# Expert blocks, token shift and weight conversions: one shift buffer for two mixes, five units in another form, a third weight chunk converted later

## The chip, the core and the metric

The kernel runs on one core of a Trainium2 chip. The metric is device time in microseconds, the median of several executions. Of the engines, TensorE appears in the profile as PE (matmuls) and PEld (weight loads), VectorE as DVE, ScalarE as ACT, GpSimd as POOL, and SyncE as SP, which issues nearly all DMAs.

## The reference

Three layers in a row, for 4 sequences of 1088 tokens: an attention with polynomial features, an expert layer with a token shift, and a gated layer with a spatial product over the tokens. All is float32.

```python
# 1 attention, 4 heads of 32: phi(x) = (S1 x) outer (S2 x), 64 features
num = einsum('bhsf,bhfd->bhsd', phi(q), kv)          # kv = sum over s of phi(k) v
x = num / (einsum('bhsf,bhf->bhs', phi(q), z) + 1e-6) # z = sum over s of phi(k)
# 2 expert layer, d 128, d_ff 1024; x_prev is x one token back
xk = mu_k * x + (1 - mu_k) * x_prev
xr = mu_r * x + (1 - mu_r) * x_prev
x = sigmoid(xr @ w_r) * (relu(xk @ w_k) ** 2 @ w_v)
# 3 gated layer
u, v = split(relu(x @ w_in))
v = einsum('ts,bsd->btd', w_spatial, normalised(v)) + b_spatial
out = (u * v) @ w_out
```

## The kernel before

Features lie on the 128 partitions and tokens along the columns. Each sequence is cut into three chunks of 384, 384 and 320 tokens, so there are twelve chunks j = 0 to 11. A float32 product is made from two parts of each operand: a high part H (a copy rounded to the type of the fast matmul) and a low part L, which is the value less H. A *split* product is three matmuls, `mm3` (L131): low by high, high by high, high by low. `copy` (L134) is an ACT pass and makes H; `low` (L137) is a subtraction on DVE or POOL and makes L. A *plain* product is one float32 matmul (L406), which the profile shows as two passes.

**Expert layer.** It runs as 96 units g = 8 j + f: eight blocks f of 128 hidden features for each of twelve chunks. `up(g)` makes a unit's first product into one of three PSUM banks (0, 1, 2, in rotation) and its Relu on ACT (L362). Then the unit is squared in one of three forms, which `kind(g)` takes from the pattern `PAT`:

- P: POOL squares the Relu (L365), ACT makes H by a second square (L394), DVE makes L. The second product is split.
- D: ACT squares into a float32 tile (L382). The second product is plain (L406), with the float32 weights `wvT`.
- Q: DVE multiplies the bank by its Relu (L370), ACT copies to H, POOL makes L. The second product is split.

From unit 26 to 85 even units are P and odd ones D. `down(g)` makes the second product four units after the first (`LAG`) and adds up over the chunk's eight units in one bank. L410 on DVE multiplies the finished chunk by the sigmoid.

**Token shift.** The tile `x` of a sequence holds a zero column and then the tokens, so the token before is the same tile one column to the left. For chunk j `prep(j)` has POOL subtract the two (L318) into the tile `mx` and DVE make the mix xk in place there (L319); then H on ACT and L on DVE. `prep_r(j)` uses `mx` again: ACT scales the token before (L335), DVE adds the other part (L336), ACT makes H and POOL makes L. There is one `mx`. The first chunk (j = 0) makes xk straight from PSUM. `receive(j)` makes the receptance product into one of the three banks of `up`, and `gate(j)` puts its sigmoid (L351) into tile m0 or m1, by j even or odd, where L410 reads it.

**Spatial weights.** They are converted in three chunks of columns, c = 0, 1, 2, with nine row blocks each. One `wstep` converts the block whose load is under way (ACT copy, low part on DVE or POOL by the table `WDVE`; the ninth also takes a second load and copy) and then issues the load of the next block (L434) into one of two tiles, `st0` and `st1`. A load of c = 2 isn't issued by a step before unit 96. `spatial(b, d, c)` are the plain units of the gated layer for the first sequence, twelve of them: four are planned among the last expert units (at 93, 95, 97, 99), eight (u = 4 to 11) follow, of which u = 4 to 7 read c = 0 and 1, and u = 8 is the first to read c = 2. `WB` says how many steps are written into each of them. Where a needed chunk isn't converted, `spatial` makes the missing steps itself first.

**Order.** `plan(g, fn, ...)` puts a helper behind unit g in the order in which the program is written. From the written program the framework's scheduler makes the order of each engine's queue, with each tile's data dependences; an instruction may run well ahead of its written place. `behind` and `late` tie a helper's instructions to earlier ones of the same engine. A tile name (`m0`, `mx`, `st0`) is one buffer: a new use waits until every reader of the old one has finished.

Of the kernel before, what the change touches and what calls it, by code (L numbers as in the profile page):

```python
# [11 lines left out]
AF = mybir.ActivationFunctionType  # L12
ALU = mybir.AluOpType
# [35 lines left out]
ES = 93  # L49
EP = 2  # L50
G2 = (86, 94)
V2 = 3
PAT = ('QD', 'PD', 'PQ', 'PD')
UT = 'x0'
# [2 lines left out]
LAG = 4  # L57
WDVE = ((0, 1), (1, 2), (2, 1), (2, 2), (3, 1), (3, 2), (4, 0), (4, 2), (6, 0), (7, 0), (7, 1), (8, 2))
VD0 = 2
WB = (0, 0, 4, 7, 2, 4, 1, 0)  # L60
NB0 = 9
W1G = 69
W1N = 8
# [21 lines left out]
def attn_moe_gmlp(ctx: ExitStack, tc: tile.TileContext, qT, kT, va, st, wk, wv, wr, win, wout,  # L85
                  wT, wtail, btail, mu, ident, msk, out):
    nc = tc.nc
    TE, VE, SE, GE = nc.tensor, nc.vector, nc.scalar, nc.gpsimd
# [7 lines left out]
    def sb(tag, shape, dt=F32):  # L96
        uid[0] += 1
        return pool.tile(shape, dt, tag=tag, bufs=1, name=f"{tag}_{uid[0]}")
# [12 lines left out]
    def m(i):  # L111
        return f"m{i}"
# [7 lines left out]

    idn = sb("idn", [128, 128])
    mk = sb("mk", [128, 24])
    mus = sb("mus", [128, 4])
    half = sb("half", [128, 1])
    ebias = sb("ebias", [128, 1])
    warm = sb("warm", [128, 1])
# [6 lines left out]
    def copy(dst, src):  # L133
        return SE.activation(out=dst, in_=src, func=AF.Copy)  # L134

    def low(eng, L, src, H):
        return eng.tensor_tensor(out=L, in0=src, in1=H.bitcast(F32), op=ALU.subtract)  # L137
# [27 lines left out]
    def load64(src, H, L, o, n):  # L165
        raw = sb(f"w{rot(*[-x for x in CVT]) * -1}", [128, n, 2], I32)
        nc.sync.dma_start(out=flat(raw), in_=src[:, o:o + n].bitcast(I32))
        pending_raw.append((raw, n, H[:, o:o + n], L[:, o:o + n]))
# [12 lines left out]
    q_s, k_s, v_s, kbd, xTs, kps, qst = {}, {}, {}, {}, {}, {}, {}  # L181
# [123 lines left out]
    anchor, prep_L, xk_op = [None, None, None], [None, None], [None]  # L305
    RA = [m(i) for i in (2, 3, 4, 5, 6, 7)]
    RB = [m(i) for i in (2, 3, 4)]
    xks, sgs, sqs, vvs, hls = {}, {}, {}, {}, {}
    x_last = [None]

    def prep(i):
        b, c = divmod(i, 3)
        o, n = CH[c]
        xT = xTs[b]
        xp = xT[:, o:o + n]
        xk = d = sb("mx", [128, n])
        if i:
            GE.tensor_tensor(out=d, in0=xT[:, o + 1:o + 1 + n], in1=xp, op=ALU.subtract)  # L318
            VE.scalar_tensor_tensor(out=xk, in0=d, scalar=mus[:, 0:1], in1=xp, op0=ALU.mult, op1=ALU.add)  # L319
        else:  # L320
            px, a = first_x
            xk_op[0] = VE.scalar_tensor_tensor(out=xk, in0=px[:, :n], scalar=mus[:, 0:1], in1=a, op0=ALU.mult, op1=ALU.add)
        H, L = sb(m(11 + i % 2), [128, n], F32R), sb(m(13 + i % 2), [128, n], F32R)
        prep_L[1] = copy(H, xk)
        if not i:
            behind(prep_L[1:], copy, xT[:, 1:1 + n], px[:, :n])
        prep_L[0] = low(VE, L, xk, H)
        xks[i] = (H, L)

    def prep_r(i):  # L330
        b, c = divmod(i, 3)
        o, n = CH[c]
        xp = xTs[b][:, o:o + n]
        xr = sb("mx", [128, n])
        SE.activation(out=xr, in_=xp, func=AF.Copy, scale=mus[:, 3:4])  # L335
        VE.scalar_tensor_tensor(out=xr, in0=xTs[b][:, o + 1:o + 1 + n], scalar=mus[:, 1:2], in1=xr, op0=ALU.mult, op1=ALU.add)  # L336
        H, L = sb("xrH", [128, n], F32R), sb("xrL", [128, n], F32R)
        copy(H, xr)
        low(GE, L, xr, H)
        sgs[i] = (H, L)  # L340
# [13 lines left out]
    def up(g):  # L354
        i, f = divmod(g, NF)
        n = CH[i % 3][1]
        hk = bank(rot(0, 1, 2))[:, :n]
        w = slice(128 * f, 128 * f + 128)
        mm3(hk, wkH[:, w], wkL[:, w], *xks[i], True, True)
        R = RA if g < GL else RB  # L360
        r = sb(rot(*R), [128, n])
        SE.activation(out=r, in_=hk, func=AF.Relu)  # L362
        if kind(g) == "P":
            sq = sb(rot(*R), [128, n])
            anchor[2] = GE.tensor_tensor(out=sq, in0=r, in1=r, op=ALU.mult)  # L365
            sqs[g] = (r, sq)
        elif kind(g) == "D":
            sqs[g] = (r, None)
        else:
            anchor[0] = VE.tensor_tensor(out=r, in0=hk, in1=r, op=ALU.mult)  # L370
            sqs[g] = (None, r)

    def kind(g):
        p = PAT[(g >= G1) + sum(g >= x for x in G2)]
        return p[g % len(p)]

# [171 lines left out]
    def spatial(b, d, c, fill, early=False):  # L548
        while not all((k, c) in done for k in range(NK + 1)):
            was = wi[0], len(pending_raw)  # L550
            wstep()
            assert was != (wi[0], len(pending_raw))
        Hs, Ls, T1, T2 = vnt[b, d]
        xH, xL = xsp[b]
        o, n = CH[c]
        cs, ds = slice(o, o + n), slice(128 * d, 128 * d + 128)
        pu = bank(7 if early else 3)[:, :n]
        mm3(pu, winH[:, ds], winL[:, ds], xH[:, cs], xL[:, cs], True, True)
        u = sb(UT if early else rot(m(0), m(1)), [128, n])
        SE.activation(out=u, in_=pu, func=AF.Relu)  # L560
        acc = bank(6 if early else rot(0, 1))[:, :n]
        for k in range(NK):
            mm3(acc, Hs[k], Ls[k], *wtile(k, c), k == 0, False, 0)
            if k == 6 and gout:
                gout.pop(0)()
            for fn in fill.get(k, ()):
                fn()
        TE.matmul(acc, lhsT=T2, rhs=wtile(NK, c)[1], start=False, stop=False)
        TE.matmul(acc, lhsT=T1, rhs=wtile(NK, c)[0], start=False, stop=True)
        VE.tensor_tensor(out=u, in0=acc, in1=u, op=ALU.mult)  # L570
        put_out(b, d, c, u, early)
# [269 lines left out]
    for n in range(NWARM):  # L841
# [8 lines left out]
                     in1=mk[:, 0:2 * NH].unsqueeze(2).to_broadcast([128, 2 * NH, 16]), op=ALU.mult)  # L850
# [32 lines left out]
    nc.sync.dma_start(out=idn, in_=ident)  # L883
    load64(*wseq[0])
    nc.sync.dma_start(out=mus[:, 0:2], in_=mu)
    GE.tensor_scalar(out=mus[:, 2:4], in0=mus[:, 0:2], scalar1=-1.0, scalar2=1.0, op0=ALU.mult, op1=ALU.add)
    load64(*wseq[1])
    load_k(1)
    load64(*wseq[2])
# [6 lines left out]
    def behind(anchors, fn, *a):  # L896
        with ExitStack() as es:
            for x in anchors:
                es.enter_context(tc.issue_after(x.ins))
            fn(*a)  # L900
# [18 lines left out]
    q_out(0)  # L919
    x_turn0 = list(x_turn)  # L920
    prep(0)
    behind([q_last], conv64, False)
    load64(*wseq[3])
# [13 lines left out]
    def plan(g, fn, *a):  # L937
        todo.setdefault(g, []).append(lambda: fn(*a))

    def gated(fn):  # L940
        return wraps(fn)(lambda *a: behind(prep_0, fn, *a))
# [4 lines left out]
    for j in range(1, NI):  # L946
        sp = 1 if j < 3 else 3 if j == 3 else 2
        for n, fn in enumerate((q_feat, q_turn, q_num, q_out)):
            plan(QS[j] + sp * n, gated(fn) if j < 3 and n == 0 else fn, j)
        e = QS[j] + 3 * sp  # L950
        plan(max(8 * j - 8, e + 1), prep, j)
        plan(max(8 * j - 6, e + 2), prep_r, j)
        plan(8 * j - 1, receive, j)
        plan(8 * j, gate, j)
    QE = [QS[3 * b + 2] + 1 for b in range(B)]
# [25 lines left out]
    for n in range(2):  # L981
        plan(R0[n], total_wv, n)
        plan(R0[n], conv_first)
    plan(R1, prep_r, 0)
    plan(R1 + 3, receive, 0)
    plan(R1 + 4, gate, 0)
# [15 lines left out]
        plan(g, late, xsplit, 0, n)  # L1002
    plan(VN[1], late, normalise, 0, 1)
    plan(NI * NF, late, normalise, 0, 2)
    for n in range(8):
        plan(GL + GW + n, wstep)
    for n in range(W1N):
        plan(W1G + n, wstep)
# [20 lines left out]
    for u, (d, c) in enumerate(ORD0):  # L1029
        if u < EARLY:  # L1030
            continue
        fill = {}

        def add(k, fn, *a):
            fill.setdefault(k, []).append(lambda: fn(*a))

        for k in range(WB[u] if u < len(WB) else 0):
            add(k, wstep)
        if u == EARLY:
            add(0, behind, [x_last[0]], xsplit, 1)  # L1040
        for n, j in enumerate({5: (0, 1), 6: (2, 3), 7: (4, 5), 8: (6, 7)}.get(u, ())):
            add(2 + 3 * n, v_rest)
            add(2 + 3 * n, v_tile, 1, j)
        for k, fn, *a in W2.get(u, ()):
            if fn == "load":
                add(k, sums_load, *a)
            else:
                add(k, held, sums, *a)
        if u == 9:
            add(2, v_rest)  # L1050
            for n in (11, 12):
                add(4, quad_load, 1, 0, n)
        if u == 10:
            add(2, tails, 1, 0, vtail[:, 0])
            for n in (22, 21):
                add(2, quad_load, 1, 0, n)
        if u == 11:
            add(1, build, 1, 0, 0)
            add(4, build, 1, 0, 1)
        spatial(0, d, c, fill)  # L1060
    assert wi[0] >= len(worder) and not pending_raw
    groups = [(b, p) for b in range(1, B) for p in range(2)]
    for gi, (b, p) in enumerate(groups):
# [7 lines left out]
        for st, _ in enumerate(group(b, p)):  # L1071
# [26 lines left out]
            if b + 1 < B:  # L1098
                if p == 0 and 0 <= st - V2 * (gi == 0) < NK:
                    v_tile(b + 1, st - V2 * (gi == 0), (3, 7))  # L1100
                elif p == 1 and st == 0 and b % 2:
# [59 lines left out]
```

## Time and profile before

| | |
|---|---|
| Time before | 452.53 us, median of 3 (452.09 to 452.95) |
| Profiled execution | 452.46 us, of which the span is 450.7 us |
| PE busy | 440.8 us (98%), 2691 matmuls |
| PEld busy | 420.4 us (93%) |
| DVE busy | 297.5 us (66%) |
| ACT busy | 270.4 us (60%) |
| POOL busy | 223.2 us (50%) |
| TensorE's granted clock | full in every slice |

Matmuls are pipelined and their ends are modelled, so a busy PE isn't PE at its peak. Idle time of an engine that is not the bottleneck costs nothing by itself. A wait for several signals is put down to the one that came last.

### The profile page before, as it was taken

Reading aid. Unit: us, or ns where it says so; the run is one execution under the profiler, and the core shown is the slowest. Engines: PE = TensorE matmul, PEld = TensorE weight load, DVE = VectorE, ACT = ScalarE, POOL = GpSimd, SP = SyncE. Lnnn points to the kernel's source line nnn. Section 1 sums busy time; section 2 is a strip of 40 time slices with the busy share of each in tenths; the row PEclk is TensorE's granted clock in tenths of the full one; section 3 lists DMA queues with packets and bytes.
Section 4 is the critical chain, followed back from the end, with each engine's and each line's share of the span. In section 5 each row is a group of like instructions: output and inputs, shape, how many; then the busy total and the mean of one; then the engine's idle time right before and its main releaser. Section 6 shows DMA issues by size and latency. Waiting matters only on the chain.

```text
span 450.7 us, 7621 instructions
## 1 busy us (share of the span) xinstructions
PE 440.8 (98%) x2691; PEld 420.4 (93%) x2691; DVE 297.5 (66%) x531; ACT 270.4 (60%) x629; POOL 223.2 (50%) x271
## 2 busy tenths in 40 slices
PE   8899999999999999999999999999999999999997
PEld 7897989989998988899999999999999999999996
DVE  5995777779864986566587797862755951734513
ACT  2595888998977898767446664334545434533322
POOL 2166477496744585868222426544435534335220
PEclk9999999999999999999999999999999999999999
DMA  7981100011100030033238422313022232010001
GB/s 232 369 297 49 51 0 2 2 52 54 27 2 0 22 120 19 19 87 113 59 117 256 131 63 93 118 54 110 15 85 93 72 110 69 19 41 25 0 2 49
DMA packets 30950, 34.92 MB, mean 77 GB/s; under 512 B 2816, under 2 KB 26432, under 8 KB 30912
## 3 DMA queue, kind: packets, MB, share of 16 engines
q1 hardware_dynamic: 30768, 34.43, 23.8%
q8 instruction: 21, 0.34, 0.3%
q14 instruction: 17, 0.14, 0.1%
q10 hardware_dynamic: 144, 0.01, 0.0%
HBM read 25.91 MB, written 8.52 MB: 76 GB/s over the span
## 4 chain that ended last, share of the span: by engine, by line
PE 84%; DVE 6%; DMA 3%; ACT 3%; POOL 1%; issue 1%; SPq 1%; ACTq 0%; DVEq 0%
PE p L131 67%; PE p L406 5%; PE p L276 3%; PE p L239 2%; PE p L208 2%; DMA w<-in_wk_dram 1%; PE p L260 1%; PE p L722 1%; PE p L721 1%; DMA st<-in_wT_dram 1%; DVE w L148 1%; DVE w L147 1%; PE p L294 1%; ACT m L362 1%; DVE mx L319 1%
## 5 line engine op out<-in xcount | busy, mean ns | idle before, releaser
L131 PE MATMUL p<-m,k 128*128 128x384 f32 (+1 forms) x288 | 65.5, 349 | 0.0
L131 PE MATMUL p<-w,k 128*128 128x384 f32 (+1 forms) x360 | 63.8, 323 | 0.0
L131 PEld LDWEIGHTS p<-w,k 128*128 128x128 f32 x360 | 59.2, 188 | 0.3
L621 DVE TENSOR_TENSOR m<-p,m 128x384 f32<-128x384 f32 (+2 forms) x37 | 18.6, 520 | 57.0 <-PE p L722 56.1
L134 ACT ACTIVATE m<-m 128x384 fp32r<-128x384 f32 (+2 forms) x49 | 24.6, 502 | 45.9 <-DVE m L735 25.6
L131 PEld LDWEIGHTS p<-m,k 128*128 128x128 f32 x288 | 48.2, 189 | 4.1
L137 POOL TENSOR_TENSOR k<-VR,k 128x512 fp32r<-128x512 f32 x25 | 34.0, 1364 | 33.4 <-ACT k L134 28.6
L362 ACT ACTIVATE m<-p 128x384 f32<-128x384 f32 (+1 forms) x96 | 43.1, 468 | 8.2 <-PE p L131 6.4
L137 DVE TENSOR_TENSOR m<-m,m 128x384 fp32r<-128x384 f32 (+1 forms) x48 | 34.3, 715 | 11.2 <-ACT m L134 8.8
L131 PE MATMUL p<-w,n1H 128*128 128x384 f32 (+1 forms) x192 | 41.1, 326 | 0.0
L365 POOL TENSOR_TENSOR m<-m 128x384 f32<-128x384 f32 (+1 forms) x35 | 30.0, 859 | 21.5 <-ACT m L362 21.0
L137 DVE TENSOR_TENSOR w<-m,w 128x384 fp32r<-128x384 f32 (+1 forms) x35 | 26.0, 746 | 15.4 <-POOL m L365 11.4
L131 PE MATMUL p<-w,n1L 128*128 128x384 f32 (+1 forms) x168 | 34.8, 324 | 0.9 <-POOL n1L L137 0.9
L134 ACT ACTIVATE m<-p 128x384 f32<-128x384 f32 (+1 forms) x36 | 17.1, 482 | 30.0 <-PE p L131 21.7
L137 POOL TENSOR_TENSOR n1H<-VR,n1H 128x512 fp32r<-128x512 f32 x12 | 15.5, 1293 | 37.1 <-ACT n1H L134 26.4
L406 PE MATMUL p<-w,wvT 128*128 128x384 f32 (+1 forms) x86 | 33.4, 470 | 0.0
L131 PEld LDWEIGHTS p<-w,n1H 128*128 128x128 f32 x192 | 32.6, 188 | 0.5
L500 POOL TENSOR_SCALAR rs<-mv 128x1 f32<-128x1 f32 x34 | 8.8, 260 | 43.3 <-DVE mv L499 42.4
L131 PEld LDWEIGHTS p<-w,n1L 128*128 128x128 f32 x168 | 28.5, 188 | 1.4 <-POOL n1L L137 1.2
L504 DVE TENSOR_SCALAR VR<-VR,mv,rs 128x512 f32<-128x512 f32 x24 | 20.5, 855 | 12.6 <-POOL rs L501 12.3
L134 ACT ACTIVATE k<-VR 128x512 fp32r<-128x512 f32 x25 | 15.7, 630 | 21.4 <-PE p L131 17.1
L131 PE MATMUL p<-w,xs1H 128*128 128x384 f32 (+1 forms) x90 | 26.9, 338 | 0.0
(288 smaller groups left out, 1212.6 us busy)
## 6 DMA issues: line engine op xcount, KB each, us to landing
vd<-VR SPq DMA_DIRECT2D x24, 256.0 KB, 2.0
VR<-vd SPq DMA_DIRECT2D x24, 256.0 KB, 2.9
st<-in_wT_dram SPq DMA_DIRECT2D x16, 192.0 KB, 2.4
w<-in_kT_dram SPq DMA_DIRECT2D x8, 192.0 KB, 4.4
w<-in_qT_dram SPq DMA_DIRECT2D x8, 192.0 KB, 4.0
VR<-in_wT_dram SPq DMA_DIRECT2D x8, 192.0 KB, 2.6
out_dram<-m SPq DMA_DIRECT2D x8, 192.0 KB, 2.1
m<-in_wT_dram SPq DMA_DIRECT2D x8, 192.0 KB, 4.5
```

The costliest lines, as they stand in the source:

```text
L131: TE.matmul(out_ap, lhsT=l, rhs=r, start=first and n == 0, stop=last and n == 2, skip_group_check=skip)
L134: return SE.activation(out=dst, in_=src, func=AF.Copy)
L137: return eng.tensor_tensor(out=L, in0=src, in1=H.bitcast(F32), op=ALU.subtract)
L208: TE.matmul(wide[:, 64 * t:64 * t + 128], lhsT=src[:, cut(c, t, CH[c][0])], rhs=Sbd, start=True, stop=True)
L239: TE.matmul(kv[:, w * g:w * g + w], lhsT=kp, rhs=vt if wide else vt[:, VP * g:VP * g + VP], start=(t == 0), stop=(t == NT - 1))
L276: nd_pe[0] = TE.matmul(o.rearrange("p h c -> p (h c)"), lhsT=qt[g][:, cut(c, t)], rhs=kb[:, g], start=not wide or g == 0, stop=not wide or ...
L362: SE.activation(out=r, in_=hk, func=AF.Relu)
L365: anchor[2] = GE.tensor_tensor(out=sq, in0=r, in1=r, op=ALU.mult)
L406: TE.matmul(vvs[i], lhsT=wvT[:, f // 2], rhs=hls.pop(g), start=f == 0, stop=f == NF - 1)
L500: GE.tensor_scalar(out=rs, in0=mv[:, 1:2], scalar1=1e-6, scalar2=None, op0=ALU.add)
L504: VE.tensor_scalar(out=v, in0=r, scalar1=mv[:, 0:1], scalar2=rs, op0=ALU.subtract, op1=ALU.mult)
L621: return eng.tensor_tensor(out=o, in0=a, in1=b_, op=op)
```

## The change

`prep` now writes POOL's difference into a tile of its own, m0 or m1 by j even or odd, and the mix into `mx`. `prep_r` makes its mix on DVE from the kept difference; ACT's scaling (L335) and the second constant in `mus` go. For the first chunk the difference is made by a subtraction that wasn't there. `prep` and `prep_r` are planned two units later, unless the query chain sets the place. Units 53, 55, 57, 59 and 61 become Q where they were D. Of the eight conversion steps planned behind units 92 to 99 the last four go; the spatial units u = 4, 5, 6, 7 get steps at their row blocks 1, 4, 7 (u = 7 at 1 and 4) where u = 4, 5, 6 had two, four and one at the first row blocks.

```diff
+KQ = (53, 55, 57, 59, 61)
...
-WB = (0, 0, 4, 7, 2, 4, 1, 0)
+WB = {4: (1, 4, 7), 5: (1, 4, 7), 6: (1, 4, 7), 7: (1, 4)}
...
-    mus = sb("mus", [128, 4])
+    mus = sb("mus", [128, 3])
...
     def prep(i):
-        xk = d = sb("mx", [128, n])
+        d = sb(m(i % 2), [128, n])
+        xk = sb("mx", [128, n])
         if i:
             GE.tensor_tensor(out=d, in0=xT[:, o + 1:o + 1 + n], in1=xp, op=ALU.subtract)
             VE.scalar_tensor_tensor(out=xk, in0=d, scalar=mus[:, 0:1], in1=xp, op0=ALU.mult, op1=ALU.add)
...
         if not i:
             behind(prep_L[1:], copy, xT[:, 1:1 + n], px[:, :n])
+            GE.tensor_tensor(out=d, in0=xT[:, o + 1:o + 1 + n], in1=xp, op=ALU.subtract)
         prep_L[0] = low(VE, L, xk, H)
         xks[i] = (H, L)
+        ds_[i] = d

     def prep_r(i):
+        d = ds_.pop(i)
         xr = sb("mx", [128, n])
-        SE.activation(out=xr, in_=xp, func=AF.Copy, scale=mus[:, 3:4])
-        VE.scalar_tensor_tensor(out=xr, in0=xTs[b][:, o + 1:o + 1 + n], scalar=mus[:, 1:2], in1=xr, op0=ALU.mult, op1=ALU.add)
+        VE.scalar_tensor_tensor(out=xr, in0=d, scalar=mus[:, 1:2], in1=xp, op0=ALU.mult, op1=ALU.add)
...
     def kind(g):
+        if g in KQ:
+            return "Q"
...
-        plan(max(8 * j - 8, e + 1), prep, j)
-        plan(max(8 * j - 6, e + 2), prep_r, j)
+        plan(max(8 * j - 6, e + 1), prep, j)
+        plan(max(8 * j - 4, e + 2), prep_r, j)
...
-    for n in range(8):
+    for n in range(4):
         plan(GL + GW + n, wstep)
...
-        for k in range(WB[u] if u < len(WB) else 0):
+        for k in WB.get(u, ()):
             add(k, wstep)
```

## Rows read from the trace of the kernel before

**Rows 1.** Busy time by stretches: stretch, length, PE, PEld, DVE, ACT, POOL, clock, DMA.

```profile
119.00:141.00 22.00, 22.00 (x148) 20.26 (x146) 14.29 (x28) 16.01 (x40) 11.72 (x16) 1.00 0.00 1
30.00:75.00 45.00, 43.24 (x288) 38.78 (x287) 33.49 (x61) 35.86 (x91) 29.86 (x28) 1.00 0.15 48
75.00:165.00 90.00, 90.00 (x558) 81.71 (x557) 68.77 (x121) 75.23 (x188) 58.49 (x70) 1.00 0.10 29
165.00:210.00 45.00, 43.37 (x242) 40.60 (x241) 28.82 (x44) 35.36 (x91) 31.17 (x34) 1.00 0.23 68
```

**Rows 2.** Waits of PE, 35 to 205 us: total us, times, longest us.

```profile
PE p L294 <- DVE VR L282: 0.7, 2, 0.4
...
PE p L406 <- ACT m L382: 0.7, 1, 0.7
...
PE p L260 <- POOL n1L L219: 0.3, 1, 0.3
```

**Rows 3.** The chain that ended last, two pieces: start us, us, what.

```profile
122.85 0.53 PE p L131 x3
123.38 0.65 PE p L406 x2
```

**Rows 4.** Groups of instructions: line, engine, tiles, shapes, count; busy us, mean ns.

```profile
L137 POOL TENSOR_TENSOR w<-m,w 128x384 fp32r<-128x384 f32 x10 | 11.3, 1129 | 8.3 <-PE p L260 7.8 <-ACT w L134 0.5
...
L319 DVE SCALAR_TENSOR_TENSOR mx<-mx,mus,x 128x384 f32<-128x384 f32 x7 | 8.5, 1217 | 4.4 <-POOL mx L318 4.4
...
L318 POOL TENSOR_TENSOR mx<-x 128x384 f32<-128x384 f32 x7 | 6.4, 911 | 1.0 <-ACT x L134 1.0
...
L137 DVE TENSOR_TENSOR m<-mx,m 128x384 fp32r<-128x384 f32 x8 | 5.9, 735 | 1.8 <-ACT m L134 1.2 <-PE p L131 0.7
...
L370 DVE TENSOR_TENSOR m<-p,m 128x384 f32<-128x384 f32 x10 | 5.5, 552 | 2.8 <-ACT m L362 2.8
...
L335 ACT ACTIVATE mx<-x,mus 128x384 f32<-128x384 f32 x8 | 4.9, 614 | 1.9 <-DVE m L137 1.9
```

**Rows 5.** Timeline, 41 to 45 us: start, us, instruction, [idle before, releaser].

```profile
41.50 0.62 ACT L335 ACTIVATE mx<-x,mus 128x384 f32<-128x384 f32 x1 [1.26 <-DVE m L137]
...
43.17 1.51 POOL L219 TENSOR_TENSOR n1L<-sab 128x768 f32<-128x768 f32 x1 [2.12 <-ACT sab L134]
```

**Rows 6.** Timeline of POOL, DVE and PE, near 58, 67 and 148 us.

```profile
58.06 1.51 POOL L219 TENSOR_TENSOR n1L<-sab 128x768 f32<-128x768 f32 x1
...
58.14 1.84 DVE L319 SCALAR_TENSOR_TENSOR mx<-mx,mus,x 128x384 f32<-128x384 f32 x1 [0.18 <-POOL mx L318]
...
67.14 0.39 PE L131 MATMUL p<-w,xs1L 128*128 128x320 f32 x1 [0.66 <-DVE de L281]
...
147.70 0.60 DVE L319 SCALAR_TENSOR_TENSOR mx<-mx,mus,x 128x384 f32<-128x384 f32 x1
```

**Rows 7.** Timeline of DVE and ACT: gates, sigmoids and one Relu.

```profile
66.44 0.55 DVE L410 TENSOR_TENSOR x<-p,m 128x384 f32<-128x384 f32 x1
...
70.60 0.49 ACT L351 ACTIVATE m<-p 128x384 f32<-128x384 f32 x1
...
92.52 0.55 DVE L410 TENSOR_TENSOR x<-p,m 128x384 f32<-128x384 f32 x1
...
98.62 0.43 ACT L351 ACTIVATE m<-p 128x320 f32<-128x320 f32 x1
...
100.28 0.43 ACT L362 ACTIVATE m<-p 128x320 f32<-128x320 f32 x1
```

**Rows 8.** Timeline of ACT near 203 and 220 us; then a piece of the chain.

```profile
202.87 0.47 ACT L134 ACTIVATE w<-st 128x320 fp32r<-128x320 f32 x1 [0.79 <-DMA st<-in_wT_dram]
203.25 0.45 ACT L382 ACTIVATE m<-m 128x320 f32<-128x320 f32 x1
...
219.92 0.47 ACT L134 ACTIVATE w<-st 64x320 fp32r<-64x320 f32 x1 [1.60 <-DMA st<-in_wtail_dram]
...
236.19 5.87 PE p L131 x36
```

More of the change, by code (lines that the diff above doesn't have):

```diff
@@ L307, in attn_moe_gmlp @@
     RB = [m(i) for i in (2, 3, 4)]
-    xks, sgs, sqs, vvs, hls = {}, {}, {}, {}, {}
+    xks, sgs, sqs, vvs, hls, ds_ = {}, {}, {}, {}, {}, {}
     x_last = [None]
@@ L885, in attn_moe_gmlp @@
     nc.sync.dma_start(out=mus[:, 0:2], in_=mu)
-    GE.tensor_scalar(out=mus[:, 2:4], in0=mus[:, 0:2], scalar1=-1.0, scalar2=1.0, op0=ALU.mult, op1=ALU.add)
+    GE.tensor_scalar(out=mus[:, 2:3], in0=mus[:, 0:1], scalar1=-1.0, scalar2=1.0, op0=ALU.mult, op1=ALU.add)
     load64(*wseq[1])
```

## The prediction

> **What bounds the kernel now.** I read the busy time by stretches first [rows 1]. From 75 to 165 us PE is busy for 90.00 of 90.00 us, while DVE has 68.77, ACT 75.23 and POOL 58.49. In that stage a microsecond taken from DVE, ACT or POOL is worth nothing by itself; only matmul work counts. PE has holes in two places: 45.00 - 43.24 = 1.76 us between 30 and 75, and 45.00 - 43.37 = 1.63 us between 165 and 210. Of what lies after 210 the change touches weight conversions alone.
>
> Next I read what PE waited for while the expert blocks run [rows 2]: 0.7 us for DVE's L282, 0.7 us for ACT's square L382, 0.3 us for a POOL outer product. These are some of the pieces of the holes above. The chain of waits [rows 3] then gives the two prices of matmul work: a split product (L131, three matmuls) 0.53 us, a plain one (L406, two passes) 0.65 us, both for 384 columns.
>
> **The change part by part.** The profiled execution took 452.46 us: 450.7 us of span and 1.76 us around it. The median shown is 452.53. I make the sum against 452.46 and add the 0.07 at the end.
>
> *Five units become Q (53, 55, 57, 59, 61).* All five belong to chunks of 384 columns. Each exchanges a plain product for a split one: 0.65 - 0.53 = 0.12 us less on PE [rows 3], 0.60 us together. They are worked on between about 119 and 141 us, where PE is busy for 22.00 of 22.00 us [rows 1], so I count all of it. Each adds a DVE multiply of 552 ns and a POOL low part of 1129 ns [rows 4], together 2.76 and 5.65 us; ACT keeps one instruction, a copy in place of a square. DVE has 22.00 - 14.29 = 7.71 us free there and POOL 22.00 - 11.72 = 10.28 [rows 1], so both additions hide. Without that cover they would come onto the path between a unit's first product and its second, which lie four units apart. Bounds: 0 (the feeding becomes the limit) and -0.60. I take -0.60.
>
> *The shift is kept, and DVE makes both mixes from it.* ACT loses L335, 12 passes of at most 614 ns on the mean [rows 4], up to 7.4 us. Between 75 and 165 us PE covers that, and it is worth nothing. It is worth something where ACT, which works in order, stood at L335: at 41.50 it had been idle for 1.26 us, since that pass writes the one buffer `mx` that a DVE low part was still reading [rows 5]. The features' copy stood behind it, and POOL sat idle for 2.12 us until its outer product at 43.17 [rows 5]. PE waited 0.3 us for an outer product of POOL's [rows 2]; this I give back. A second hole, 0.66 us before the product at 67.14, follows a DVE queue in which the third chunk's mix took 1.84 us at 58.14 [rows 6]; that mix moves away (next part), so I give this back too. That makes 1.0 us. But the order on every engine is laid anew when the kernel is built, so I take 0.70. Bounds: 0 and the whole hole, -1.76. The receptance's mix stays one DVE instruction with two buffers as inputs. The first chunk gets one more subtraction on POOL, 911 ns [rows 4]; nothing but the receptance's mix, planned five units later, waits for it. Without that cover it costs its 0.9 us once. The smaller `mus` costs nothing.
>
> *The shift lives in m0 and m1, and the plan moves it by two units.* The sigmoid of the block before last sits in the same buffer, and L410 reads that last. So the subtraction for chunk j can't start before L410 of chunk j-2 has ended: 66.44 + 0.55 = 66.99 us for chunk 3 and 92.52 + 0.55 = 93.07 for chunk 5 [rows 7]. Subtraction, mix and low part take 0.91 + 1.22 + 0.74 us [rows 4], the copy on ACT about 0.47 as the copy at 202.87 [rows 8]: 3.3 us. Chunk 5 is ready at 96.4, and the first Relu of its block stood at 100.28 [rows 7], so 3.9 us are left, less the first product's own 0.53. I cost this at nothing; without that cover the block's start is late by what the chain exceeds it. What is late next is the receptance, whose mix follows in the same `mx`: 0.60 (the mix at 147.70 [rows 6]) + 0.47 + 1.13 = 2.2 us more, so 98.6 for chunk 5 and 72.5 for chunk 3. Their sigmoids stood at 98.62 and 70.60 [rows 7], with a product of 0.53 ahead of each: chunk 5 is 0.5 us late and chunk 3 some 2.4 us. PE has other work ready then, so I cost this at nothing too, with the price under the last rival.
>
> *Weight conversions of the third chunk.* Four planned steps leave units 96 to 99; the two of the fifth spatial unit, the four of the sixth and the one of the seventh become three in each of these and two in the eighth. A step is an ACT copy, a low part on POOL or DVE and a load on SP; the last one has a second load and copy. Before, ACT stood for such a load right ahead of the last square: a copy at 202.87 had waited 0.79 us for its load, the square came at 203.25 [rows 8], and PE waited its 0.7 us [rows 2]. If the copies come later, that hole closes. But their data dependences stay, and these already let the copies run ahead of the place where they are written. I take half, -0.35; bounds 0 and -0.70. On SP the loads now fall among the raw loads for the sums. A delay of one spatial unit, about 7 us, is covered: the chunk's last copy stands at 219.92, and the products that read it begin after 236.19 [rows 8].
>
> **Sum:** -0.60 - 0.70 - 0.35 = -1.65, so 450.81 by the profiled execution and 450.9 by the median.
>
> **A rule against it.** DVE's mix of two buffers took 1.84 us at 58.14, beside an outer product that POOL ran from 58.06, and 0.60 us at 147.70 [rows 6]. The Trainium skill says (SBUF — State Buffer, Who interferes with whom) that a DVE instruction with two inputs in SBUF contends with a POOL instruction that reads SBUF. The trace agrees in these two rows. By that rule the change would come out as the rival in which DVE is the bound, at 452.7, and without it at 450.9.
>
> **Rivals.** *Only the matmul work shrinks.* The holes stay, at the old places or at new ones: 452.53 - 0.60 = 451.9. For it: only 1.0 + 0.7 of the 3.4 us of holes hang on what is removed or moved. Against it: the queue behind L335 [rows 5].
>
> *DVE becomes the bound over the five units.* If each of the five new POOL low parts holds a DVE instruction up for its whole length, as the outer product did with the mix in rows 6, DVE needs 14.29 + 2.76 + 5.65 = 22.70 us in a stretch of 22.00. The five products then gain nothing and 0.70 us are added: 452.53 + 0.70 = 453.2 with no hole closed, 452.2 with those of the forecast closed; the middle is 452.7. It decides once DVE's sum passes 22.00 - 0.60 = 21.40. Against it: every low part would have to meet a DVE instruction.
>
> *The receptance product holds a bank (slower).* It takes one of the three banks through which the units' first products rotate; when its operands are late, the unit that has that bank next waits. They are late by 2.4 us in chunk 3 and 0.5 in chunk 5 without queueing; with 1.26 us of queueing each, what ACT's queue lost at 41.50 [rows 5], by 3.7 + 1.8 = 5.5 us. Against that stand second products that wait to be run, say one of each kind per block, 2 x 1.18 = 2.4 us [rows 3]. That leaves 3.1 - 0.6 = +2.5 us: 455.0. It decides once the lateness passes that 1.2 us in a block. For it: the lock on m0 and m1. Against it: sums, features and value tiles fill PE there as well.
>
> **How the numbers follow.** Chances: the forecast 0.56, only matmul work 0.18, DVE the bound 0.10, the bank held 0.16. About 0.2%, 0.9 us, is what a measurement of this kernel can tell from no change, so faster means under 451.6 and slower over 453.4. The forecast lies on the faster side, the next two rivals (451.9 and 452.7) within, the last beyond: faster 0.56, same 0.28, slower 0.16. The range begins at the forecast's bound, 452.53 - 0.60 - 1.76 - 0.70 = 449.5, and ends at 453.4, above the first two rivals; the third is what it leaves out. The predicted time is the forecast's, 450.9, and its own range is 449.5 to 451.9.
>
> **What would show each step.** In the profile after, L335's group is gone, L318 has 12 instructions, L406 has ten passes fewer on PE and L131 fifteen matmuls more, and L370 has five more. PE is still busy without a hole from 75 to 165 us. Between 30 and 75 us it comes to 44 of 45 us, with shorter waits behind the outer product near 43 us and near 67 us. The last block's square doesn't follow a copy that waited for its load. The prediction is wrong if PE has a hole at a block's first unit or behind a receptance product, if DVE has no idle time left between 119 and 141 us, or if the spatial units of the third chunk wait for a conversion.

## The result, and the profile after

The changed kernel takes 455.15 us (median of 4 runs, 455.14 to 456.36) against 452.67 for the kernel before (452.09 to 452.95), where 450.9 was forecast. The ratio on record is 1.0067, 95% interval 1.0054 to 1.0079; it is estimated over the single runs, and the two medians alone give 1.0055, or 2.5 us. Either way the kernel is slower by well over the 0.2% that can be told from no change. The profiled execution took 455.16 us, with a span of 453.2 us.

Line numbers are shifted in the kernel after. The subtraction of the shift is L320, the first mix L321, the receptance's mix L340, `mm3` L132, `copy` L135, `low` L138, the sigmoid L355, the Relu L366, the DVE multiply L374, the D square L388, the plain product L412 and the gate L416.

The busy time by stretches, with the columns of [rows 1], of the kernel after:

```profile
30.00:75.00 45.00, 43.53 (x290) 39.20 (x289) 33.30 (x59) 33.15 (x85) 28.98 (x27) 1.00 0.15 45
75.00:165.00 90.00, 89.53 (x559) 81.82 (x559) 71.29 (x129) 72.00 (x182) 63.46 (x75) 1.00 0.10 27
119.00:141.00 22.00, 21.80 (x149) 20.22 (x147) 18.20 (x32) 14.85 (x37) 16.91 (x19) 1.00 0.00 1
165.00:210.00 45.00, 42.88 (x231) 38.34 (x231) 28.59 (x41) 33.75 (x85) 30.12 (x32) 1.00 0.22 64
```

Read the count of matmuls as well as PE's busy time. From 165 to 210 us PE starts 231 matmuls where it started 242 [rows 1], and it is busy for 0.49 us less. From 75 to 165 us it was busy without a hole; now 0.47 us are missing. The granted clock is 1.00 in all four stretches, before and after, so the clock is no part of this. DVE from 119 to 141 us stands at 18.20 of 22.00 us.

What PE waited for between 150 and 215 us, kernel after (total, times, longest):

```profile
PE p L132 <- DVE w L138: 0.7, 1, 0.7
PE p L132 <- ACT w L400: 0.6, 1, 0.6
PE p L132 <- DVE m L138: 0.3, 1, 0.3
PE p L132 <- ACT m L366: 0.2, 1, 0.2
PE p L412 <- ACT m L388: 0.2, 1, 0.2
```

The last row answers to the 0.7 us in [rows 2]: that wait for the last square shrank to 0.2 us. The kernel before had one other wait in this stretch, which is gone (kernel before):

```profile
PE p L131 <- POOL n1L L137: 0.9, 1, 0.9
```

The others are new. Two of them in the timeline (start, length, instruction, idle before and what ended it), with the DVE instruction that PE waited for and the ACT instructions ahead of the Relu:

```profile
165.88 0.52 ACT L135 ACTIVATE w<-st 128x384 fp32r<-128x384 f32 x1 [2.04 <-DMA st<-in_wT_dram]
166.31 0.47 ACT L366 ACTIVATE m<-p 128x384 f32<-128x384 f32 x1
...
166.84 0.80 PE L132 MATMUL p<-m,k 128*128 128x384 f32 x3 [0.19 <-ACT m L366]
...
168.15 1.26 DVE L138 TENSOR_TENSOR w<-m,w 128x384 fp32r<-128x384 f32 x1 [1.15 <-ACT w L400]
...
169.46 0.44 PE L132 MATMUL p<-w,xs1H 128*128 128x384 f32 x1 [0.74 <-DVE w L138]
```

They are the last units of chunk 9's block. ACT stood 2.04 us for the load of a spatial weight, and the Relu came right behind that copy. PE waits for the Relu at 166.84; DVE waits for ACT's copy of a squared operand at 168.15, and PE at 169.46 for the low part that DVE then makes. The next block, chunk 10's, could not fill the hole: its shift is subtracted at 170.5 and its first Relu comes at 176.4 us. That subtraction waited for its x, long after its gate had ended (158.61), so this hole is not the lock's wait itself.

**The lock.** All instructions of the subtraction (first fence) and of the mix behind it (second), kernel after: first the durations and the starts, then what ended the idle time of their engine (total us, times), then who waited for them.

```profile
L320 POOL TENSOR_TENSOR m<-x x11: 716/823/1269, 37.2 to 176.7; 128x384 f32<-128x384 f32 x7, 128x320 f32<-128x320 f32 x4
...
  DVE x L416: 2.4, 3
...
  DVE mx L321: 10.3, 7
```

```profile
L321 DVE SCALAR_TENSOR_TENSOR mx<-m,mus,x x11: 550/1096/1366, 38.0 to 177.5; 128x384 f32<-128x384 f32 x7, 128x320 f32<-128x320 f32 x4
...
  POOL m L320: 10.3, 7
```

Where POOL had nothing else to do, it stood three times for the gate L416; where it had, it did that first, and the wait shows on DVE: seven mixes found DVE idle for the subtraction, 10.3 us in all, of which 2.56 us are chunk 1's, in front of which no gate stands (2.57 in the kernel before). Before, it was 4.4 us in all [rows 4]. Chunks 5 and 6 in the timeline of DVE and POOL, kernel after:

```profile
89.18 0.55 DVE L416 TENSOR_TENSOR x<-p,m 128x384 f32<-128x384 f32 x1
...
89.81 0.72 POOL L320 TENSOR_TENSOR m<-x 128x320 f32<-128x320 f32 x1 [1.34 <-DVE x L416]
...
90.56 0.55 DVE L321 SCALAR_TENSOR_TENSOR mx<-m,mus,x 128x320 f32<-128x320 f32 x1 [0.83 <-POOL m L320]
...
102.17 0.54 DVE L416 TENSOR_TENSOR x<-p,m 128x384 f32<-128x384 f32 x1
...
102.80 1.00 POOL L320 TENSOR_TENSOR m<-x 128x384 f32<-128x384 f32 x1 [0.69 <-DVE x L416]
```

The gate ends at 89.73 and the subtraction starts at 89.81; the next gate ends at 102.71, and the subtraction starts at 102.80. From chunk 2 on, nine of the ten subtractions start within 1.2 us of that gate's end (chunk 10's, which waits for its x, does not). The prediction had this order. What it had wrong is the price.

### The profile page after: what moved, and what is told of

Same layout as the page of the kernel before. It is cut to its first block, busy times and chain, and to the rows that moved or that the text cites. A ratio compares the mean times of both kernels' runs of the same rounds, so it can differ in the third digit from the quotient of the medians.

```text
span 453.2 us, 7601 instructions
## 1 busy us (share of the span) xinstructions
PE 442.6 (98%) x2696; PEld 420.7 (93%) x2696; DVE 301.0 (66%) x536; ACT 264.2 (58%) x617; POOL 229.2 (51%) x277
## 4 chain that ended last, share of the span: by engine, by line
PE 57%; DVE 19%; ACT 8%; POOL 7%; issue 4%; DMA 4%; SPq 1%; ACTq 0%; POOLq 0%; DVEq 0%
PE p L132 51%; DVE w L138 3%; DVE m L138 2%; PE p L412 1%; POOL m L369 1%; DMA w<-in_wk_dram 1%; POOL w L138 1%; ACT m L366 1%; DVE w L149 1%; PE p L728 1%; PE p L727 1%; DVE mx L321 1%; DVE mx L340 1%; DVE w L148 1%; ACT m L135 1%
## 5 line engine op out<-in xcount | busy, mean ns | idle before, releaser
L132 PE MATMUL p<-m,k 128*128 128x384 f32 (+1 forms) x288 | 66.8, 351 | 0.6 <-DVE m L374 0.4
L132 PE MATMUL p<-w,k 128*128 128x384 f32 (+1 forms) x360 | 63.6, 323 | 0.0
L132 PEld LDWEIGHTS p<-w,k 128*128 128x128 f32 x360 | 59.2, 188 | 0.3
L132 PEld LDWEIGHTS p<-m,k 128*128 128x128 f32 x288 | 48.3, 189 | 5.1 <-DVE m L374 1.0
L135 ACT ACTIVATE m<-m 128x384 fp32r<-128x384 f32 (+2 forms) x49 | 24.6, 504 | 46.9 <-DVE m L741 25.6
L138 POOL TENSOR_TENSOR k<-VR,k 128x512 fp32r<-128x512 f32 x25 | 34.0, 1363 | 32.7 <-ACT k L135 27.9
L366 ACT ACTIVATE m<-p 128x384 f32<-128x384 f32 (+1 forms) x96 | 43.4, 472 | 3.4 <-PE p L132 2.9
L138 DVE TENSOR_TENSOR m<-m,m 128x384 fp32r<-128x384 f32 (+1 forms) x48 | 35.0, 730 | 10.3 <-ACT m L135 8.9
L132 PE MATMUL p<-w,n1H 128*128 128x384 f32 (+1 forms) x192 | 41.3, 327 | 0.0
L138 DVE TENSOR_TENSOR w<-m,w 128x384 fp32r<-128x384 f32 (+1 forms) x35 | 25.1, 725 | 16.6 <-POOL m L369 10.1
L132 PE MATMUL p<-w,n1L 128*128 128x384 f32 (+1 forms) x168 | 34.8, 324 | 0.0
L135 ACT ACTIVATE m<-p 128x384 f32<-128x384 f32 (+1 forms) x36 | 17.1, 482 | 30.2 <-PE p L132 21.9
L138 POOL TENSOR_TENSOR n1H<-VR,n1H 128x512 fp32r<-128x512 f32 x12 | 15.5, 1292 | 36.8 <-ACT n1H L135 32.5
L132 PEld LDWEIGHTS p<-w,n1H 128*128 128x128 f32 x192 | 32.7, 188 | 0.6
L132 PE MATMUL p<-w,xs1H 128*128 128x384 f32 (+1 forms) x100 | 29.6, 338 | 0.9 <-DVE w L138 0.7
L412 PE MATMUL p<-w,wvT 128*128 128x384 f32 (+1 forms) x76 | 29.4, 468 | 0.0
L132 PEld LDWEIGHTS p<-w,n1L 128*128 128x128 f32 x168 | 28.5, 188 | 0.5
L135 ACT ACTIVATE k<-VR 128x512 fp32r<-128x512 f32 x25 | 15.7, 631 | 21.4 <-PE p L132 17.1
```

The costliest lines, as they stand in the source:

```text
L132: TE.matmul(out_ap, lhsT=l, rhs=r, start=first and n == 0, stop=last and n == 2, skip_group_check=skip)
L412: TE.matmul(vvs[i], lhsT=wvT[:, f // 2], rhs=hls.pop(g), start=f == 0, stop=f == NF - 1)
```

## The experiments

Ratios are to the kernel before, with the 95% interval; the kernel before took 452.34, 452.42, 452.30 and 452.38 us as the median beside the four groups of runs (e1 to e4, e5 to e8, e9 to e12, e13 to e15). The ratios are estimated over the single runs and can differ from the ratio of two medians by 0.1%, in e13 by 0.2%.

The expectations weigh theories by number. Theory 1: the wait for the gate's buffer (the lock) is the loss. Theory 2: DVE and POOL become the bound over the five split units. Theory 3: the moved weight steps are the loss. Theory 4: the plan's two units. Theory 5: both mixes on DVE. Theory 6: the lock is one part, and the rest comes of the new order that the scheduler makes. The bank theory is the prediction's third rival.

**One part alone.** *e1* is the kernel before with the five split units and nothing else:

```
+KQ = (53, 55, 57, 59, 61)
...
+        if g in KQ:
+            return "Q"
```

> The kernel before with units 53, 55, 57, 59 and 61 as Q, nothing else. If the wait for the gate's buffer is the loss (theory 1), the split alone gains its matmul work: 0.6 us less than before, about 452.0. If DVE and POOL become the bound over these five units (theory 2), it is slower than before by 1 us or more. If the moved weight steps are the loss (theory 3), also 452.0.

Measured: 451.44 us, 0.9982 [0.9972, 0.9992]; theory 2 is out. *e2* is the kernel before with the new places of the weight steps alone:

```
-WB = (0, 0, 4, 7, 2, 4, 1, 0)
+WB = {4: (1, 4, 7), 5: (1, 4, 7), 6: (1, 4, 7), 7: (1, 4)}
...
-    for n in range(8):
+    for n in range(4):
         plan(GL + GW + n, wstep)
```

> The kernel before with the four conversion steps moved from units 96 to 99 into the spatial units, nothing else. Theory 1 and theory 2: within 0.7 us of before, 452.0 to 452.7. Theory 3 (the moved steps are the loss): 454 or more, with PE waiting near 200 us or in the spatial units.

Measured: 452.39 us, 1.0007 [0.9997, 1.0017]. *e3* is the kernel before with the kept shift in m0 and m1, both mixes from it, and the plan two units later: the whole diff without `KQ` and with the weight steps where they were.

> The kernel before with the kept shift in m0 and m1, both mixes on DVE and the plan two units later; no split units, weight steps as before. Theory 1: the loss is here, 0.6 us beyond the whole change since the split's gain is missing: about 455.8. Theory 2 or 3: 452 to 453.

Measured: 454.64 us, 1.0058 [1.0045, 1.0071]. So the loss comes with the shift, as theory 1 had it; it had 455.8, since it took the split's gain to be there in the whole change. By itself the split is worth what it was costed at, and the weight steps nothing. What PE waited for between 200 and 280 us in e2:

```profile
PE p L406 <- ACT m L382: 0.6, 1, 0.6
PE p L131 <- ACT m L134: 0.5, 1, 0.5
```

The wait for the last square stays at 0.6 us (0.7 in [rows 2]), and a second one of 0.5 us is there too.

**The plan.** *e6* moves `prep` and `prep_r` by two units in the kernel before, and nothing else:

```
-        plan(max(8 * j - 8, e + 1), prep, j)
-        plan(max(8 * j - 6, e + 2), prep_r, j)
+        plan(max(8 * j - 6, e + 1), prep, j)
+        plan(max(8 * j - 4, e + 2), prep_r, j)
```

> The kernel before with both parts of the token shift planned two units later, buffers and engines as before. Theory 4: 454 to 455. Theory 1 and 5: within 0.7 us of before, 451.8 to 453.

Measured: 452.37 us, 0.9998 [0.9989, 1.0007], span 450.8 us. The two units by themselves are worth nothing, and theory 4 is out.

**The lock alone.** *e5* is the kernel before, with ACT's scaling pass and the old plan, and only the place of the shift changed:

```
-        xk = d = sb("mx", [128, n])
+        d = sb(m(i % 2), [128, n]) if i else None
+        xk = sb("mx", [128, n])
```

> The kernel before, its scaling on ACT and its plan kept, but the shift is written into m0 or m1 in place of mx, so that the subtraction waits for the gate of the block before last. Theory 1 (the wait for the gate's buffer is the loss): about the loss of the shift-only kernel, 454 to 455. Theory 4 (the loss needs the plan's two units): 452.5. Theory 5 (the loss comes of both mixes on DVE): 452.5.

Measured: 454.02 us, 1.0042 [1.0028, 1.0056], as theory 1 had it and against 4 and 5. The subtraction (L319 in e5) and what ended POOL's idle time ahead of it, and below that the busy time from 30 to 165 us, in e5:

```profile
L319 POOL TENSOR_TENSOR m<-x x11: 712/822/1137, 36.7 to 179.0; 128x384 f32<-128x384 f32 x7, 128x320 f32<-128x320 f32 x4
...
  DVE x L411: 10.4, 7
```

```profile
30.00:75.00 45.00, 44.27 (x298) 40.05 (x297) 30.88 (x58) 36.00 (x92) 28.70 (x28) 1.00 0.15 47
75.00:165.00 90.00, 88.16 (x537) 78.32 (x535) 66.45 (x121) 72.61 (x182) 56.42 (x68) 1.00 0.10 28
```

POOL stood 10.4 us for the gate (L411 here), and PE, which had no hole from 75 to 165 us [rows 1], lost 1.84 us there and started 21 matmuls fewer. Ten of these it had started earlier, from 30 to 75 us (298 against 288), and from 165 to 210 us it starts 246 against 242, so by 210 us it is 7 behind. PE's busy time over these 180 us doesn't show the loss at all (176.77 us against 176.61). In the source nothing but the buffer differs from the kernel before.

**The lock taken away.** *e9* is the whole change, but the shift lies in two other buffers, m8 and m9, which nothing else uses until unit 88. *e11* is the same without the split and with the old weight steps, *e10* with the split, the old plan and the old weight steps.

```
-        d = sb(m(i % 2), [128, n])
+        d = sb(m(8 + i % 2), [128, n])
```

> The whole change, but the shift in m8 and m9, which nothing else uses between the first microseconds and unit 88. Theory 1 (waiting for a buffer is the whole loss): faster than before, 450.5 to 451.7, with subtractions that start right after the copy of x. Theory 6 (the lock is one part, the rest comes of the new order that the scheduler makes): 451.8 to 453. Theory 5 (both mixes on DVE are the loss): 454 or more.

> Five split units and both mixes on DVE with the shift in m8 and m9; plan and weight steps as before. Theory 1: 450 to 451.4, under the split alone. Theory 6: 451.5 to 452.7. Theory 5: 453.5 or more.

> Both mixes on DVE with the shift in m8 and m9, no split units, weight steps as before. Theory 1: at or under before, 451.3 to 452.5. Theory 6: 452.5 to 453.5. Theory 5: near the shift-only kernel's 454.6.

Measured: e9 452.30 us, 0.9998 [0.9987, 1.0008]; e10 451.95, 0.9996 [0.9985, 1.0008]; e11 452.08, 0.9993 [0.9982, 1.0004]. e9 and e10 lie where theory 6 had them and above theory 1's gain, e11 lies where theory 1 had it, and theory 5 is out. The mix in e9, and e9's busy time by stretches:

```profile
L321 DVE SCALAR_TENSOR_TENSOR mx<-m,mus,x x11: 528/618/1343, 38.2 to 173.1; 128x384 f32<-128x384 f32 x7, 128x320 f32<-128x320 f32 x4
...
  POOL m L320: 3.5, 2
```

```profile
30.00:75.00 45.00, 42.91 (x285) 38.77 (x283) 33.48 (x57) 32.47 (x84) 29.42 (x29) 1.00 0.15 48
75.00:165.00 90.00, 89.95 (x568) 82.89 (x567) 76.07 (x131) 74.06 (x188) 65.11 (x74) 1.00 0.10 28
165.00:210.00 45.00, 43.90 (x243) 41.13 (x243) 26.92 (x42) 32.85 (x86) 29.43 (x33) 1.00 0.22 66
```

The mix waits 3.5 us in two places instead of 10.3 in seven. From 30 to 210 us PE starts 285 + 568 + 243 = 1096 matmuls, after the change 290 + 559 + 231 = 1080, so the kernel with the lock is 16 behind by then. One name of a buffer is 1.0067 - 0.9998 = 0.0069 of 452.5 us, 3.1 us; without the split it is 1.0058 - 0.9993 = 0.0065, 2.9 us. By the medians, each against its own kernel before, it is 2.5 us in both pairs.

**A shorter lock.** *e4* and *e7* put the shift into `xrL`, the receptance's own low part, from chunk 2 on. It comes free when the receptance product of the chunk before has run, much earlier than the gate. e4 is the whole change with it, e7 only the shift's part, and *e8* has the split with the old plan and the old steps.

```
-        d = sb(m(i % 2), [128, n])
+        d = sb("xrL" if i > 1 else m(i), [128, n])
```

> The whole change, but from the third chunk on the shift is put into the buffer of the receptance's low part, which is free from the receptance product of the chunk before; the subtraction then need not wait for the gate of the block before last. Theory 1: the loss goes, 451 to 452.5, and the subtractions start several us ahead of where the gate two blocks before would let them. Theory 2 or 3: stays near 455.

> The shift-only kernel (both mixes on DVE, plan two units later, no split units, weight steps as before) with the shift in the receptance's low part from the third chunk on. Theory 1: back to before or a little under, 451.5 to 452.7. Theory 4 and 5: near the shift-only kernel's 454.6.

> A version that may beat both: five split units, both mixes on DVE, the shift in the receptance's low part, the plan and the weight steps as before. Theory 1: the split's 0.9 us remain and the freed ACT passes may add to it, 450.5 to 451.5. Theory 5: above 453.

Measured: e4 452.74 us, 1.0007 [0.9999, 1.0016]; e7 454.01, 1.0034 [1.0022, 1.0047]; e8 452.70, 1.0002 [0.9993, 1.0012]. In e4 the subtractions of chunks 4 to 6 start at 72.17, 85.61 and 98.89 us, some 4 us earlier than after (76.3, 89.81 and 102.80). e7 lies clearly between its kernel with the lock on the gate's buffer (e3, 1.0058) and without a lock (e11, 0.9993); e4 and e8 lie well under 1.0067, but their intervals overlap those of e9 and e10, so they don't show that a shorter lock still costs. e4 came 0.2 us above theory 1's range; e8 missed the gain that theory 1 gave it, and e7 missed theory 1's range altogether. e7, without the split and with the old weight steps, is slower than e4 by 1.3 us; I have no explanation for it.

**Which way the late shift costs.** The third rival said that the receptance product holds a bank while its operands are late. *e12* is the whole change with that product planned two units later, meant to start when its operands are there; *e13*, *e14* and *e15* are the same move in the kernel before, in e9 and in e5.

```
-        plan(8 * j - 1, receive, j)
-        plan(8 * j, gate, j)
+        plan(8 * j + 1, receive, j)
+        plan(8 * j + 2, gate, j)
```

> The whole change in m0 and m1, but the receptance product and its gate are planned two units later, behind two more units in the rotation of the three banks. If the late receptance operands cost through the held bank (the third rival's way), much of the 2.7 us comes back: 452.5 to 453.7. If they cost another way (ACT and DVE standing in order for the late mix), it stays at 454.5 to 455.8.

> The kernel before, with the receptance product planned at unit 8j+1 and the gate at 8j+2, two units later than it was; nothing else. If the 1.9 us that came back in the run with the whole change and the later receptance came from a bank that the late receptance product no longer holds, then here, where its operands are not late, the move is worth nothing: within 0.2% of before, 452.3 +- 0.9. If the move is a better order by itself, about 450.5 (faster by 0.3 to 0.5%). If it costs something by itself, over 453.2, and the recovery of the bank's price was then larger than 1.9 us.

> The whole change with the shift in m8 and m9 (no lock by the gate), and the receptance two units later as above. Bank theory: the operands are not late, so the move is worth nothing against the same kernel with the receptance at its old place (0.9998 of before): 452.3 +- 0.9. Better order by itself: about 450.5. Costs by itself: over 453.2.

> The kernel before with its shift written into m0 and m1 alone (454.02 without the move, 1.0042), and the receptance two units later. Bank theory: most of the lock's 1.7 us comes back, 452.3 to 452.9. If the late mix itself, and ACT and DVE that stand in order for it, is what costs: no gain, 453.5 to 454.5, or more, since the gate and with it the release of the buffer come later.

Measured: e12 453.55 us, 1.0025 [1.0013, 1.0037]; e13 457.04, 1.0086 [1.0052, 1.0121]; e14 453.04, 1.0011 [0.9997, 1.0026]; e15 453.08, 1.0010 [0.9996, 1.0023].

| kernel | at the old place | two units later | the move |
|---|---|---|---|
| lock, whole change | 1.0067 | 1.0025 (e12) | -0.0042 = -1.9 us |
| lock alone | 1.0042 (e5) | 1.0010 (e15) | -0.0032 = -1.4 us |
| no lock, whole change | 0.9998 (e9) | 1.0011 (e14) | +0.0013 = +0.6 us |
| before | 1 | 1.0086 (e13) | +0.0086 = +3.9 us |

By the medians the four moves are -1.2, -0.9, +0.7 and +4.7 us. The move pays only where the buffer is locked. The runs of this last group scatter more (the kernel before from 451.23 to 454.36 us), and the intervals of e9 and e14 overlap, so +0.6 us may be nothing. e12 came where the bank theory had it, and e15 between the two forecasts. e13 missed the 452.3 that the bank would give. The longest wait of PE in it, and the busy time just behind, with the columns of [rows 1]:

```profile
69.19 1.17 PE L131 MATMUL p<-m,k 128*128 128x320 f32 x3 [2.69 <-DVE m L370]
```

```profile
70.00:75.00 5.00, 5.00 (x31) 4.84 (x30) 3.36 (x6) 2.84 (x7) 1.39 (x2) 0.74 0.01 3
```

A single unit's multiply stopped PE for 2.69 us. The trace shows why it came late: from 63.23 to 68.21 us DVE ran five steps of a weight's conversion (L144 to L149), ACT stood 1.29 us for one of them with the unit's Relu behind it (67.42), and the multiply came at 68.66. Right after PE had stood, its granted clock was 0.50, the 1.2 GHz level, until 72.6 us. Five of e13's seven runs have a mean clock of 0.993 to 0.996 and took 455.20 to 459.27 us; the two at 1.000 took 454.40 and 455.19. So the lowered clock is part of e13's loss, and at the full clock the move costs some 2.4 us (an estimate from these two runs and the 452.38 of before). The hole comes of where the scheduler put a weight's conversion, so e13 says little about the bank.

## Why the prediction was wrong

**The step that failed** is "The shift lives in m0 and m1, and the plan moves it by two units", and in it the two sentences "I cost this at nothing" and "PE has other work ready then, so I cost this at nothing too". The times in that paragraph were right or too careful: it had chunk 5's subtraction at 93.07 us and its operand at 96.4, and they came at 89.81 and 93.8; the lateness that it worked out for the sigmoids, without queueing, was 2.4 us in chunk 3 and 0.5 in chunk 5. The price was wrong: about 3 us and not 0 (e9 and e11 against the same kernels with the lock; e5 alone gives 0.0042, 1.9 us). At the two chunks that the paragraph works out, 3 and 5, PE did have other work, as the rows below show. What it left out is the rest: the lock held from chunk 2 on, and with it the scheduler made another order, in which PE runs short elsewhere.

**The third rival had the time and the lateness, but the trace does not show its price where it put it.** It gave 455.0 us, from 3.7 us of lateness in chunk 3 and 1.8 in chunk 5. The receptance product of chunk 3 and its sigmoid in the kernel after, PE and ACT:

```profile
70.17 0.34 PE L132 MATMUL p<-xrH,wrL 128*128 128x384 f32 x1
70.34 0.34 PE L132 MATMUL p<-xrH,wrH 128*128 128x384 f32 x1
...
72.63 0.42 PE L132 MATMUL p<-xrL,wrH 128*128 128x384 f32 x1
...
74.35 0.48 ACT L355 ACTIVATE m<-p 128x384 f32<-128x384 f32 x1
```

The same in e9:

```profile
68.69 0.34 PE L132 MATMUL p<-xrH,wrL 128*128 128x384 f32 x1
...
69.04 0.34 PE L132 MATMUL p<-xrL,wrH 128*128 128x384 f32 x1
...
70.65 0.49 ACT L355 ACTIVATE m<-p 128x384 f32<-128x384 f32 x1
```

In e9 the three matmuls start within 0.35 us and the bank is free at 71.1. In the kernel after the low part `xrL` is ready at 70.8, after the first two; the third stands behind other work in PE's order, and the bank is taken from 70.17 to 74.8. The sigmoid is 74.35 - 70.60 = 3.75 us later than in [rows 7], where the rival had 3.7; in chunk 5 it stands at 100.0, 1.4 us later, where the rival had 1.8. So the lateness is shown. Its price is not there. From 65 to 105 us, over both late receptances, PE starts as many matmuls in the kernel after as before (first row after, second before; e9 starts 245):

```profile
65.00:105.00 40.00, 39.83 (x244) 35.96 (x243) 30.42 (x52) 35.58 (x90) 28.21 (x31) 1.00 0.07 21
```

```profile
65.00:105.00 40.00, 39.33 (x242) 35.55 (x240) 31.69 (x54) 35.02 (x86) 29.96 (x30) 1.00 0.07 21
```

The matmuls are missing from 165 to 175 us (after, before, e9):

```profile
165.00:175.00 10.00, 9.06 (x45) 7.32 (x45) 7.18 (x10) 6.71 (x16) 5.13 (x5) 1.00 0.31 92
```

```profile
165.00:175.00 10.00, 10.00 (x54) 9.20 (x53) 7.47 (x11) 8.97 (x23) 6.54 (x8) 1.00 0.25 76
```

```profile
165.00:175.00 10.00, 10.00 (x53) 9.20 (x53) 8.53 (x13) 6.56 (x18) 6.47 (x7) 1.00 0.27 80
```

That is the hole behind ACT's wait for a load, shown with the result. Chunk 9's block had started earlier than before (first Relu at 155.60 against 157.81 us), and chunk 10's starts 3.1 us later (176.42 against 173.36). In e3, the shift alone, the hole lies in the same stretch (46 matmuls), but there no load takes ACT longer than 0.5 us, so the load is not the whole of it.

For the bank speaks that moving the product brings 1.4 to 1.9 us back with the lock and nothing without it, and that e5 starts only 94 matmuls from 85 to 105 us (121 before), beside the receptance products of chunks 4 and 5, which are spread over 1.9 and 2.7 us. Against it: e15, where chunk 4's product runs in one piece, starts only 90 there; and the kernel before had 2.06 us between the first and the last matmul in chunk 7 and 1.65 in chunk 9, without a hole in PE. The block's own operand needs the same shift too, and for chunk 6 it is 10.3 us later than in the kernel before (109.3 against 99.0 us), with 4.9 us between two units' Relus at that block's start against 3.4. So that the lock costs some 3 us is shown by the runs; how its wait gets to PE stays open, and that the rival's 455.0 lies so near to 455.15 has to be called luck.

**The split, -0.60 us.** Right by itself: e1 gained 0.0018 of 452.34, 0.8 us (0.4 to 1.3). It did not add to the rest: with the shift in m8 the kernel with the split and the one without it (e10 and e11, 0.9996 and 0.9993; they differ in the plan too, which e6 found to be worth nothing) can't be told apart. PE's page lines of after and of e9, total over the span:

```profile
PE 442.6 (98%) x2696; PEld 420.7 (93%) x2696; DVE 301.0 (66%) x536; ACT 264.2 (58%) x617; POOL 229.2 (51%) x277
```

```profile
PE 440.4 (98%) x2696; PEld 421.6 (94%) x2696; DVE 304.2 (68%) x536; ACT 263.2 (58%) x617; POOL 229.6 (51%) x277
```

**The holes in front, -0.70 us.** They moved and did not close. PE is busy for 43.53 of the 45 us from 30 to 75, 43.24 before [rows 1], not the 44 that I wanted to see; in e9 it is 42.91. The rows of DVE, ACT, POOL and PE near 42 us, kernel after:

```profile
41.19 0.62 DVE L340 SCALAR_TENSOR_TENSOR mx<-m,mus,x 128x384 f32<-128x384 f32 x1
...
41.72 0.22 DVE L282 RECIPROCAL de<-de 128x12 f32<-128x12 f32 x1
...
41.84 0.53 ACT L135 ACTIVATE xrH<-mx 128x384 fp32r<-128x384 f32 x1 [1.15 <-DVE mx L340]
...
41.98 0.56 DVE L283 TENSOR_TENSOR VR<-p,de 128x384 f32<-128x384 f32 x1
...
42.68 0.52 PE L295 MATMUL p<-idn,VR 128*128 128x128 f32 x3 [0.85 <-DVE VR L283]
...
43.41 1.51 POOL L220 TENSOR_TENSOR n1L<-sab 128x768 f32<-128x768 f32 x1
...
43.48 1.85 DVE L340 SCALAR_TENSOR_TENSOR mx<-m,mus,x 128x384 f32<-128x384 f32 x1 [0.95 <-POOL xrL L138]
```

ACT no longer stands for `mx` at its scaling pass, but 1.15 us for the mix, one instruction further on (1.26 at L335 in [rows 5]). The wait of 0.30 us for POOL's outer product is gone, as forecast. But the mix no longer waits for ACT, so it slips in on DVE ahead of the reciprocal at 41.72, and PE waits 0.85 us for L283 behind it, where the longest such wait was 0.4 us [rows 2]. The second hole, 0.66 us ahead of the product at 67.14, is gone as well. So both waits that the term gave back did go, and others took their place: that is the first rival, new holes for old ones. e11, the shift without a lock and without the split, came to 0.9993, -0.3 us [-0.8, +0.2]: the freed ACT passes are worth nothing that can be measured.

**The weight steps, -0.35 us.** Nothing: e2 1.0007, and e9 against e10 0.9998 to 0.9996. The last square still waits where only the steps moved (e2), and it no longer does in e3, whose steps are at the old place; a wait of 0.5 us for an ACT copy stands near 275 us in e2 and after. I had halved the term for the reason that now holds in full: the copies run where their data let them.

**DVE as the bound** was rightly put low. From 119 to 141 us DVE went from 14.29 to 18.20 us, +3.91; the five multiplies of 549 ns make 2.7 of it, and 3.8 us of the stretch remained free. The mix at 43.48 took 1.85 us beside the outer product from 43.41, and the one at 41.19, with POOL idle, 0.62 us. The Trainium skill (SBUF — State Buffer, Who interferes with whom) has a DVE instruction with two inputs in SBUF contend with a POOL instruction that reads SBUF, and these two rows agree.

**A reading that was off.** The row for L282 in [rows 2] is that of the whole span; from 35 to 205 us PE waited for it 0.4 us, once. And the longest wait of that stretch, 0.9 us for a POOL low part at 181.57 us, is not among the three that the prediction read. No term of the sum rests on either.

**The sum as it should have been:** e9 at 0.9998 says that everything but the lock is worth -0.1 us (-0.6 to +0.4), not -1.65, and the lock adds 3.1. The only kernel that is clearly faster than the kernel before is e1, the split units alone, at 0.9982.

## What to carry to other kernels

A buffer "of its own" that shares its name with a longer-lived tile is a wait on that tile's last reader: follow the lock to the operand that it delays, and if that operand is later than its reader stood before, price it, even if the engine that reads it seems to have other work. Where a spare buffer can be had, run the kernel with it: here that showed the price, which no single wait in the trace did. Time a change's parts alone before they go together: here the split alone was worth -0.8 us, the shift as it was written cost 2.6, and only the first was worth keeping. An engine that is freed off the path gives nothing, and the instruction that was waiting for it may slip ahead of one on the path.

## What the runs showed of the hardware

PE's busy time isn't its work: after and e9 run the same 2696 matmuls, and PE is busy for 442.6 and 440.4 us. Of the 3.1 us between the spans (453.2 and 450.1) only 0.9 us show as idle time of PE, so the idle time that a stretch shows can be less than what it has lost. From 165 to 210 us the matmuls that PE starts (231 against 243) and the busy time of the weight loads (PEld, 38.34 against 41.13 us) tell it better.
